# Decay attention with a squared-ReLU MLP: whole heads' reciprocals through POOL's queue, division one unit sooner, and another pace of weight conversion

## The chip, the cores and the metric

The kernel runs on one core of a Trainium2 chip. The metric is the device time of the program in microseconds (us), as the median of several runs; less is better. The core has five engines with instruction queues of their own, each worked off in order: PE (matrix products), DVE (vector), ACT (scalar functions), POOL (GpSimd) and SP, which here only issues DMA transfers.

## The reference, cut to what matters

```python
def _attn_ref(q, k, v, f):            # (8, 8, 576, 64), f: (8, 8, 576)
    scores = np.matmul(q, k.transpose(0, 1, 3, 2)) / np.sqrt(D)
    cum = np.cumsum(np.log(np.clip(f, 0.0001, 1.0)), axis=-1)
    scores = np.where(causal, -1e9, scores + cum[..., :, None] - cum[..., None, :])
    scores = scores - np.max(scores, axis=-1, keepdims=True)
    attn = np.exp(scores)
    attn = attn / (np.sum(attn, axis=-1, keepdims=True) + 1e-09)
    return np.matmul(attn, v)
...
x = attn_out.transpose(0, 2, 1, 3).reshape(8 * 576, 512)
h = np.maximum(x @ w_in, 0.0)         # w_in: (512, 2048), float64
return (h * h @ w_out)                # w_out: (2048, 512), float64
```

There are 8 batches of 8 heads, so 64 heads of 576 positions, and an MLP over 4608 rows.

## The kernel before

**Units.** Each head is cut into 6 *units* (a block of keys against a range of queries). The 384 units, numbered n = 0 to 383, are written out in one long loop, which starts at n = -12 to prepare. In unit n the loop writes the scores and the exponential of that unit (PE, then ACT, line 409), the product with the values of the unit two before (PE, lines 435 to 437 or 456), and then whatever falls due in that unit. The row maxima of the next head (PE line 346, DVE line 354) are among this. `in_order` at the end fixes the order of tracing on PE, ACT, DVE and POOL, so each engine works in exactly this order. SP's queue is left to the order in which its transfers are written.

**Whole and split heads.** The first 14 heads (`NWHOLE`, units 0 to 83) are "whole": their operands stay float32, and PE passes over each matrix product several times. The others are "split" into a high and a low part of reduced precision, which costs work on DVE (lines 313, 314, 332, 425), ACT (line 424) and POOL (lines 321, 324, 333, 411) and saves PE passes.

**Division.** The sum of each row's exponentials comes out of the value product as one more row. Two heads (a pair) share a tile `den` of 128 partitions. `finish` divides in four parts: part 0 loads the two rows from `den` into the compact tile `cmp` (128 partitions by 9), part 1 forms the reciprocal on DVE and stores it to a DRAM tile `rdr`, part 2 spreads each head's 576 reciprocals over its 64 partitions of `den` with two transfers, and part 3 multiplies the tile `xt` with `den` on POOL (line 492). All transfers are on SP's queue. `DIVIDE` says how many units behind the pair's last unit each part is written: 2, 5, 8 and 11 for the first 8 heads, and 2, 4, 6 and 7 for the others.

**Conversion of weights.** The MLP's 32 weight tiles arrive as float64. `weight_ops` turns each into a float32 and then a high and a low part, in four steps per tile: `tensor_scalar` on DVE (line 228); `tensor_scalar` on DVE (line 233) and the high part of the tile before on ACT (line 210); `scalar_tensor_tensor` on DVE (line 236), the low part of the tile before on POOL (line 216) and the magnitude of the next on ACT (line 205); `scalar_tensor_tensor` on DVE (line 240) and the next loads on SP (line 194). There are 132 steps. `RATES` says how many steps a unit gets: 1 in units -12 to -7, 1.6 in -3 to -1, 0.8 from unit 0 to `ready[0]`, and 2 behind it. The tile `osb` that a conversion writes has two buffers, so line 233 of a tile waits until POOL has read the tile two before.

**MLP.** `ready[b]` is the unit from which batch b's rows may be used, two behind the division of its last pair. `split_x` (DVE lines 509 and 510) splits 256 rows at a time. `fill` writes the MLP's steps between the units, each step in two halves: `mlp1` (12 products on PE, line 522, then ACT lines 530 and 532, DVE lines 531 and 533) and, for the step before, `mlp2` (6 products on PE, line 545). The 64 halves of the first two chunks are spread evenly up to `ready[1]`, which is 104. A step can only be written once its two weight tiles are converted; when chunk 0 lacks weights, chunk 1 goes on with those that are there. Once the last tile is converted, the halves that are left are spread anew.

Of the kernel before, what the change touches and what calls it, by code (L numbers as in the profile page):

```python
# [34 lines left out]
def decay_attention_relu2_kernel(  # L35
# [18 lines left out]
    nc = tc.nc  # L54

    NH, D, _, S = qk.shape
# [17 lines left out]
    NWHOLE = 14  # L74
# [8 lines left out]
    def bank(use):  # L83
# [11 lines left out]
        out=mz[:, MW - P:], in_=mz[:, MW - P:], pattern=[[-1, P]],  # L95
# [6 lines left out]
        out=eye, in_=eye, pattern=[[-1, P]],  # L102
# [370 lines left out]
    def finish(h, part):  # L473

        st = state[h]
        den = st["den"]
        if part == 0:
            st["cmp"] = wk.tile([P, S // D], F32, name="cmp")

            for i in range(2):  # L480
                nc.sync.dma_start(out=st["cmp"][i * D:(i + 1) * D], in_=den[i * D:i * D + 1, :])
        if part == 1:
            nc.vector.tensor_scalar_add(st["cmp"], st["cmp"], EPS)
            nc.vector.reciprocal(out=st["cmp"], in_=st["cmp"])
            st["rdr"] = dr.tile([2, S], F32, name="rdr")
            nc.sync.dma_start(out=st["rdr"].rearrange("h (p c) -> (h p) c", p=D), in_=st["cmp"])
        if part == 2:
            for i in range(2):
                nc.sync.dma_start(out=den[i * D:(i + 1) * D], in_=st["rdr"][i:i + 1].broadcast_to([D, S]))
        if part == 3:  # L490
            x = xts[h // H][:, (h % H) // 2, :]
            nc.gpsimd.tensor_tensor(out=x, in0=x, in1=den, op=ALU.mult)
            del state[h], state[h - 1]
# [97 lines left out]

    RATES = (1, 1.6, 0.8, 2)
    LAG = 2
    NA = H * NU


    DIVIDE = (2, 5, 8, 11), (2, 4, 6, 7)
    MAXIMA = (0, 0.5, 1, 1.5, 2, 2.5), (1.5, 2, 2.5, 3, 3.5, 4)  # L600
    SPLIT = 0, 1, 1, 3
    LOAD = 4
# [9 lines left out]
    def fin(h, part):  # L612

        return (h + 1) * NU - 1 + DIVIDE[h >= H][part]

# [33 lines left out]
    def cv(k):  # L649
        owed[0] += k  # L650
        convert(int(owed[0]))
        owed[0] -= int(owed[0])
# [52 lines left out]
    for n in range(-2 * NU, last_slot + 1):  # L705
        live = 0 <= n < len(slots)
        split_last()
        if live:
            h, u = slots[n]
            score(h, u)  # L710
            if h >= NWHOLE:
                unsplit.append((h, u))
        for ha, ua in avs.get(n, ()):
            if ua < NU - 1:
                av_part(ha, ua, False)
            else:
                av_part(ha, ua, True)
                av_part(ha, ua - 1, True)
        for args in fins.get(n, ()):
            finish(*args)  # L720
        for do in events.get((n, 0), ()):
            do()
        wr = RATES[0] * (n < -NU) if n < -NU // 2 else RATES[1 if n < 0 else 2 if n < ready[0] else 3]
        cv(wr / 2)
        fill(n, 0.5)
        for do in events.get((n, 1), ()):
            do()
        cv(wr / 2)
        fill(n, 1.0)
# [44 lines left out]
```

## Time and profile before

| | |
|---|---|
| time, median of 3 runs | 1230.48 us (1229.43 to 1232.88) |
| the profiled execution | 1229.0 us, span 1227.3 us |
| PE busy | 1187.9 us, 97% of the span |
| PE weight loads busy | 1047.9 us, 85% |
| DVE busy | 781.5 us, 64% |
| ACT busy | 710.3 us, 58% |
| POOL busy | 376.4 us, 31% |
| DMA | 71.88 MB, mean 59 GB/s |

A profile's "busy" is the time in which the engine has an instruction under way; overlapping instructions count once. PEclk is the share of full speed that the TensorE clock was granted. In a list of groups, "x12 | 15.5, 1290 | 22.4 <-ACT w L210 22.4" means: twelve instructions, 15.5 us busy, 1290 ns mean, 22.4 us idle on this engine just before them, and what ended the idle time. In a timeline a row is the start, the duration, the engine, the line, the operation and its tiles.

### The profile page before, as it was taken

The page shows a single profiled execution, that of the slowest core. Times are in us where ns is not written, and L with a number is a line of the kernel's source. Part 1 is how long each engine was busy: PE and PEld are TensorE (multiplying, and loading weights), DVE is VectorE, ACT ScalarE, POOL GpSimd, SP SyncE. Part 2 cuts the span into 40 slices and gives each one's busy share as a digit, 9 for nine tenths or more (in the row PEclk, how much of TensorE's full clock was granted, in tenths as well). Part 3 has the DMA queues.
Part 4 walks back from the last instruction along what each step waited for, and adds up shares of the span by engine and source line. Part 5 has one row for each costly group of instructions (what it writes and reads, how often), then busy time and mean ns, then how long its engine had stood idle before and what let it go on. Part 6 is the DMA issues. An engine that isn't in the chain of part 4 may idle for free.

```text
span 1227.3 us, 23243 instructions
## 1 busy us (share of the span) xinstructions
PE 1187.9 (97%) x7770; PEld 1047.9 (85%) x7770; DVE 781.5 (64%) x2046; ACT 710.3 (58%) x1748; POOL 376.4 (31%) x566
## 2 busy tenths in 40 slices
PE   6997998899999999999999999999999999999998
PEld 3665877788999899999999989998999899999997
DVE  5767778876666767666665666767666667533322
ACT  2774655556666666665656666666666666533232
POOL 3332234533333333332322243333333433200000
PEclk8998999899999999999999999999999999999999
DMA  7777501121221212111111121211111212000000
GB/s 216 209 187 178 185 16 33 25 70 34 48 50 41 59 41 53 37 44 36 49 19 56 26 59 42 58 41 45 38 52 41 59 41 59 11 28 1 18 18 18
DMA packets 106376, 71.88 MB, mean 59 GB/s; under 512 B 88184, under 2 KB 88184, under 8 KB 106256
## 3 DMA queue, kind: packets, MB, share of 16 engines
q1 hardware_dynamic: 105136, 66.26, 21.0%
q0 software_dynamic: 1120, 4.13, 1.4%
q8 instruction: 62, 1.02, 0.4%
q14 instruction: 58, 0.48, 0.1%
HBM read 60.20 MB, written 9.88 MB: 57 GB/s over the span
## 4 chain that ended last, share of the span: by engine, by line
PE 76%; ACT 2%; issue 2%; POOL 1%; DVE 0%; DVEq 0%; POOLq 0%
PE bank L522 30%; PE bank L545 28%; PE bank L435 3%; PE bank L437 3%; PE bank L402 3%; PE bank L436 3%; PE bank L346 3%; PE bank L399 3%; POOL v L333 0%; ACT den L471 0%; ACT p L409 0%; ACT r L530 0%; ACT ph L424 0%; ACT gh L532 0%; POOL p L411 0%
## 5 line engine op out<-in xcount | busy, mean ns | idle before, releaser
L545 PE MATMUL bank<-w,gh 128*128 128x512 f32 x1152 | 412.9, 399 | 0.0
L522 PE MATMUL bank<-xh,w 128*128 128x256 f32 x2304 | 331.5, 287 | 5.5 <-DVE tcol L354 5.5
L522 PEld LDWEIGHTS bank<-xh,w 128*128 128x128 f32 x2304 | 303.5, 191 | 13.2 <-DVE tcol L354 5.9
L425 DVE TENSOR_TENSOR pl<-p,ph 128x320 fp32r<-128x320 f32 (+4 forms) x300 | 186.0, 620 | 196.9 <-ACT ph L424 191.4
L545 PEld LDWEIGHTS bank<-w,gh 128*128 128x128 f32 x1152 | 217.1, 188 | 38.1
L530 ACT ACTIVATE r<-bank 128x256 f32<-128x256 f32 x288 | 110.3, 383 | 220.3 <-PE bank L522 200.3
L545 PE MATMUL bank<-w,gl 128*128 128x512 f32 x576 | 226.8, 394 | 0.1
L531 DVE TENSOR_TENSOR g<-r 128x256 f32<-128x256 f32 x288 | 128.5, 446 | 139.0 <-ACT r L530 138.3
L411 POOL TENSOR_SCALAR_AFFINE_SELECT p<-p 128x128 f32<-128x128 f32 (+1 forms) x250 | 83.6, 334 | 423.6 <-ACT p L409 322.7
L424 ACT CAST ph<-p 128x320 fp32r<-128x320 f32 (+4 forms) x300 | 124.4, 415 | 152.3 <-POOL p L411 110.2
L522 PE MATMUL bank<-xl,w 128*128 128x256 f32 x1152 | 185.6, 284 | 0.0
L522 PEld LDWEIGHTS bank<-xl,w 128*128 128x128 f32 x1152 | 159.3, 192 | 0.0
L533 DVE TENSOR_TENSOR gl<-g,gh 128x256 fp32r<-128x256 f32 x288 | 134.4, 467 | 35.7 <-DVE g L531 0.9
L409 ACT ACTIVATE p<-bank 128x320 f32<-128x320 f32 (+4 forms) x300 | 115.9, 386 | 62.7 <-PE bank L402 51.2
L354 DVE CUSTOM_DVE_ANT_0 bank<-bank,mz 128x256 f32<-128x256 f32 (+4 forms) x320 | 133.5, 432 | 27.4 <-PE bank L346 23.3
L346 PE MATMUL bank<-rk 66*128 66x320 f32 (+4 forms) x384 | 112.5, 318 | 22.0 <-DVE tcol L354 13.4
L532 ACT ACTIVATE gh<-r 128x256 fp32r<-128x256 f32 x288 | 120.4, 418 | 9.2
L545 PEld LDWEIGHTS bank<-w,gl 128*128 128x128 f32 x576 | 109.0, 189 | 14.3 <-DVE gl L533 0.9
L346 PEld LDWEIGHTS bank<-rk 66*128 66x128 f32 (+1 forms) x384 | 68.2, 182 | 40.1 <-DVE tcol L354 16.5
L435 PE MATMUL bank<-pl,vh 128*65 128x320 f32 (+4 forms) x350 | 97.6, 279 | 4.6 <-ACT den L471 4.6
L436 PE MATMUL bank<-ph,v 128*64 128x320 f32 (+4 forms) x350 | 95.2, 272 | 0.0
L437 PE MATMUL bank<-ph,vh 128*65 128x320 f32 (+4 forms) x350 | 93.8, 274 | 0.0
(85 smaller groups left out, 1523.5 us busy)
## 6 DMA issues: line engine op xcount, KB each, us to landing
qkraw<-in_qk SPq DMA_DIRECT2D x50, 288.0 KB
v<-in_v SPq DMA_DIRECT2D x64, 160.0 KB
den<-rdr SPq DMA_DIRECT2D x64, 144.0 KB
out<-osb SPq DMA_DIRECT2D x36, 256.0 KB
w<-in_w_in SPq DMA_DIRECT2D x16, 512.0 KB
w<-in_w_out SPq DMA_DIRECT2D x16, 512.0 KB
rl<-in_qk SPq DMA_DIRECT2D x14, 288.0 KB
rk<-in_qk POOLq DMA_DIRECT2D x14, 288.0 KB, 5.0
```

The lines of the kernel that those rows point to most:

```text
L346: nc.tensor.matmul(ps[:m, :n], st["r2"][:D + 2, q0:q0 + m], st["kl0"][:D + 2, k0:k0 + n], start=True, stop=True,)
L354: nc.vector.tensor_tensor_reduce(out=ps[:m, :n], in0=ps[:m, :n], in1=mz[:m, mo:mo + n], op0=ALU.add, op1=ALU.min, scale=-1.0, scalar=init, ...
L424: nc.scalar.copy(out=ph[:kn, :n], in_=p[:kn, :n])
L425: nc.vector.tensor_tensor(out=pl[:kn, :n], in0=p[:kn, :n], in1=ph[:kn, :n].bitcast(F32), op=ALU.subtract,)
L435: nc.tensor.matmul(acc[:D + 1, o], vh, pl[:kn, i], start=first, stop=False)
L436: nc.tensor.matmul(acc[:D, o], vl, ph[:kn, i], start=False, stop=False)
L437: nc.tensor.matmul(acc[:D + 1, o], vh, ph[:kn, i], start=False, stop=last)
L522: nc.tensor.matmul(ph[:, :T], w[:, s, cc], x[:, cc, :], start=(cc == 0 and k == 0), stop=(cc == NCC - 1 and k == 2),)
L531: nc.vector.tensor_tensor(out=g, in0=r, in1=r, op=ALU.mult)
L532: nc.scalar.activation(out=gh, in_=r, func=AF.Square)
L533: nc.vector.tensor_tensor(out=gl, in0=g, in1=gh.bitcast(F32), op=ALU.subtract)
L545: nc.tensor.matmul(po, g[:, ts], w[:, s], start=(fc == 0 and k == 0), stop=(fc == NF - 1 and k == 2),)
```

## The change

`finish` takes POOL's queue instead of SP's for the store of part 1 and the two transfers of part 2, for the 14 whole heads (7 pairs). For the first 8 heads parts 1, 2 and 3 are written one unit sooner: 4, 7 and 10 units behind the pair's last. With this `ready[0]` goes from 60 to 59, and so do the split of the first rows and the MLP's first step. Conversion gets 1.1 steps a unit from unit 0 to 58 and 2.3 from unit 59.

```diff
@@ finish
         den = st["den"]
+        queue = nc.gpsimd if h < NWHOLE else nc.sync
...
-            nc.sync.dma_start(out=st["rdr"].rearrange("h (p c) -> (h p) c", p=D), in_=st["cmp"])
+            queue.dma_start(out=st["rdr"].rearrange("h (p c) -> (h p) c", p=D), in_=st["cmp"])
         if part == 2:
             for i in range(2):
-                nc.sync.dma_start(out=den[i * D:(i + 1) * D], in_=st["rdr"][i:i + 1].broadcast_to([D, S]))
+                queue.dma_start(out=den[i * D:(i + 1) * D], in_=st["rdr"][i:i + 1].broadcast_to([D, S]))
...
-    RATES = (1, 1.6, 0.8, 2)
+    RATES = (1, 1.6, 1.1, 2.3)
...
-    DIVIDE = (2, 5, 8, 11), (2, 4, 6, 7)
+    DIVIDE = (2, 4, 7, 10), (2, 4, 6, 7)
```

Lines behind 476 carry a number that is one higher in the changed kernel. By the rates, the 132 steps end in unit 95 before (1 ahead of the loop, 10.8 up to unit -1, 48 in units 0 to 59, the other 72.2 at 2) and in unit 83 now (1, 10.8, 64.9 in units 0 to 58, the other 55.3 at 2.3).

**Ahead of the MLP's first step.** On POOL before, heads 6 and 7 (the last pair of batch 0, tile `den_914`) leave one row; `w..` are weight tiles, `rk` is a head's rounded operands, `v` its values.

```order
L216 TENSOR_TENSOR w11_1051<-osb_970,w11_1051 128x512
L216 TENSOR_TENSOR w12_1135<-osb_1049,w12_1135 128x512
L303 MEMSET v_1154 128x5x2
L287 DMA rk_0_79<-in_qk 64x1152
L492 TENSOR_TENSOR xt0_333<-xt0_333,den_914 128x576
L216 TENSOR_TENSOR w13_1213<-osb_1133,w13_1213 128x512
```

On POOL now, the same pair (`den_953`):

```order
L487 DMA rdr_1111<-cmp_1074 128x9
L287 DMA rk_1_80<-in_qk 64x1152
L216 TENSOR_TENSOR w15_1117<-osb_1040,w15_1117 128x512
L490 DMA den_953<-rdr_1111 64x576 x2
L216 TENSOR_TENSOR w16_1170<-osb_1115,w16_1170 128x512
L303 MEMSET v_1202 128x5x2
L493 TENSOR_TENSOR xt0_340<-xt0_340,den_953 128x576
```

The store stands ahead of a load of operands and a low part, the spread ahead of another low part, and the division behind it; four more weight tiles have been converted by then.

**At the first split head's units.** On DVE before, around unit 84; the last chunk of conversion stands between the work of the split heads (`pl<-p,ph`, `rk<-qkraw`) and of the MLP (`g`, `gl`).

```order
L531 TENSOR_TENSOR g<-r 128x256
L533 TENSOR_TENSOR gl<-g,gh 128x256
L228 TENSOR_SCALAR wmag<-wmag 128x512
L233 TENSOR_SCALAR osb<-wmag 128x512
L425 TENSOR_TENSOR pl<-p,ph 128x320
L313 CAST rk_80<-qkraw 64x576
L314 CAST rk_80<-qkraw 64x576
L236 SCALAR_TENSOR_TENSOR osb<-w_1899,osb 128x512
L531 TENSOR_TENSOR g<-r 128x256
L533 TENSOR_TENSOR gl<-g,gh 128x256
L240 SCALAR_TENSOR_TENSOR osb<-w_1899,osb 128x512
```

On DVE now, at the same place:

```order
L532 TENSOR_TENSOR g<-r 128x256
L534 TENSOR_TENSOR gl<-g,gh 128x256
L425 TENSOR_TENSOR pl<-p,ph 128x320
L532 TENSOR_TENSOR g<-r 128x256
L534 TENSOR_TENSOR gl<-g,gh 128x256
L313 CAST rk_80<-qkraw 64x576
L314 CAST rk_80<-qkraw 64x576
L354 ISA bank_2289,tcol<-bank_2289,mz 128x256
```

The four conversion rows have gone from here and from the eleven units behind; they stand between the whole heads' maxima now.

## The prediction

> **What bounds the kernel now.** I read the page first: engines, then the slices.
>
> ```profile
> PE 1187.9 (97%) x7770; PEld 1047.9 (85%) x7770; DVE 781.5 (64%) x2046; ACT 710.3 (58%) x1748; POOL 376.4 (31%) x566
> PE   6997998899999999999999999999999999999998
> PEclk8998999899999999999999999999999999999999
> ```
>
> PE bounds the program. The change takes nothing from PE, so it can only win idle PE time and clock, and both are missing in the first 9 slices alone. So I cut that part by unit: the exponentials of line 409 give the start of units 0, 60, 66, 84, 96 and 108 at 26.9, 105.3, 131.9, 192.2, 240.5 and 278.7 us. The first row below counts 61 of them (units 0 to 59, and one at the edge).
>
> ```profile
> 26.90:105.30 78.40, 23.28 (x61) 1.00 0.79 201
> ```
>
> All engines in these stages:
>
> ```profile
> core 0: us, PE busy (x) PEld busy (x) DVE busy (x) ACT busy (x) POOL busy (x), PEclk, DMA share, GB/s
> 26.90:105.30 78.40, 73.86 (x415) 48.50 (x414) 56.98 (x175) 56.79 (x141) 25.94 (x35) 1.00 0.79 201
> 105.30:131.90 26.60, 20.77 (x123) 17.12 (x121) 18.72 (x40) 11.63 (x29) 5.89 (x7) 0.87 0.67 185
> 131.90:192.20 60.30, 58.22 (x357) 47.66 (x356) 44.96 (x103) 33.73 (x82) 19.97 (x17) 1.00 0.24 74
> 192.20:240.50 48.30, 41.10 (x246) 36.09 (x245) 41.19 (x87) 27.83 (x68) 24.41 (x27) 0.93 0.13 30
> 240.50:278.70 38.20, 34.54 (x223) 30.95 (x224) 27.03 (x67) 22.60 (x58) 14.56 (x21) 0.96 0.20 57
> 278.70:311.10 32.40, 32.03 (x221) 29.22 (x220) 22.04 (x61) 20.71 (x53) 11.87 (x19) 1.00 0.19 40
> 311.10:1227.30 916.20, 910.49 (x6133) 829.62 (x6131) 556.85 (x1485) 530.34 (x1316) 264.94 (x414) 1.00 0.16 40
> ```
>
> Behind 278.7 us PE idles 6 us in 949, and the order there doesn't change. Two stages lose much: units 60 to 65 (the MLP's start) and units 84 to 95 (the first two split heads), where DVE is busy 41.19 of 48.3 us.
>
> **Units 84 to 95.** Two steady split heads take 32.4 us (row 278.70) with 16 MLP halves. Here 17.5 halves are due by the code (64 x 12/44), and the chain of waits prices a half:
>
> ```profile
> 1035.20 1.47 PE bank L545 x6
> 1037.06 1.50 PE bank L522 x12
> ```
>
> So PE needs 32.4 + 1.5 x 1.5 = 34.6 us and takes 48.3: 13.7 us are lost. The groups of DVE in this stage name the cause:
>
> ```profile
> L240 DVE SCALAR_TENSOR_TENSOR osb<-w,osb 128x512 int32<-128x512 int32 x6 | 7.8, 1292 | 0.1
> L236 DVE SCALAR_TENSOR_TENSOR osb<-w,osb 128x512 int32<-128x512 int32 x6 | 4.1, 676 | 0.0
> L228 DVE TENSOR_SCALAR wmag<-wmag 128x512 f32<-128x512 f32 x6 | 3.6, 604 | 0.0
> L233 DVE TENSOR_SCALAR osb<-wmag 128x512 int32<-128x512 int32 x6 | 3.5, 591 | 0.1
> ```
>
> Six weight tiles are converted here: 7.8 + 4.1 + 3.6 + 3.5 = 19.0 of DVE's 41.2 us. The new rates end the conversion in unit 83, so DVE keeps 22.2 us of work, as in the steady row (22.04). The nearest rows for what loss stays are the steady stage (0) and units 96 to 107, without conversion but with the banks of this stage: 38.2 - 34.6 = 3.6 us. I take 3, nearer to the second, whose banks are the same. Gain: 13.7 - 3 = **10.7 us** (10.1 to 13.7).
>
> The stage behind (240.5) has a clock of 0.96: 0.04 x 38.2 = **1.5 us**, which I count as won too, since it is the tail of the idle time ahead of it (0 to 3.6).
>
> **What the six tiles cost where they go.** Units 0 to 58 get 0.3 x 59 / 4 = 4.4 tiles more, and units 59 to 83 the other 1.6. The price of a tile in units 0 to 59:
>
> ```profile
> L216 POOL TENSOR_TENSOR w<-osb,w 128x512 fp32r<-128x512 f32 x12 | 15.5, 1290 | 22.4 <-ACT w L210 22.4
> L236 DVE SCALAR_TENSOR_TENSOR osb<-w,osb 128x512 int32<-128x512 int32 x12 | 14.6, 1221 | 0.2
> L346 PE MATMUL bank<-rk 66*128 66x320 f32 (+4 forms) x60 | 21.1, 399 | 3.7 <-DVE p L354 3.5
> L240 DVE SCALAR_TENSOR_TENSOR osb<-w,osb 128x512 int32<-128x512 int32 x12 | 8.2, 680 | 0.1
> L228 DVE TENSOR_SCALAR wmag<-wmag 128x512 f32<-128x512 f32 x11 | 5.3, 485 | 0.0
> L233 DVE TENSOR_SCALAR osb<-wmag 128x512 int32<-128x512 int32 x12 | 5.0, 418 | 0.3
> ```
>
> The means add up to 1.22 + 0.68 + 0.49 + 0.42 = 2.80 us, so DVE gets 4.4 x 2.80 = 12.4 us more and goes from 57.0 to 69.4 of about 77 us: 90% busy. All of it could hide, or all of it could end on PE: 0 to 12.4 us. That 90% can hide, two heads of this stage show:
>
> ```profile
> 42.70:49.80 7.10, 7.01 (x42) 4.50 (x40) 6.48 (x19) 5.65 (x16) 2.41 (x5) 1.00 0.85 237
> 49.80:57.00 7.20, 7.19 (x43) 4.77 (x42) 6.35 (x17) 5.68 (x16) 1.84 (x2) 1.00 0.76 204
> ```
>
> DVE is busy 6.48 of 7.10 and 6.35 of 7.20 us while PE idles 0.1. But over the stage PE idles 78.4 - 73.9 = 4.5 us for 12 tiles, nearly all behind DVE's maxima (row L346): 0.38 us a tile, 4.4 x 0.38 = 1.7. To this come DVE's waits for `cmp`, whose load now has two units to land instead of three, in four pairs at up to half a microsecond. I take **4 us lost**, in the lower third since the nearest rows are those two heads. The 1.6 tiles behind unit 58 cost at the same rate (0.9 a tile) **1.5 us** (0 to 4.5, which is 1.6 x 2.80); DVE is busy 63.7 of 86.9 us there.
>
> **The MLP's start.** The timeline around 100 us:
>
> ```profile
> 96.03 0.22 DVE L484 RECIPROCAL cmp<-cmp 128x9 f32<-128x9 f32 x1
> ...
> 102.15 0.68 DVE L240 SCALAR_TENSOR_TENSOR osb<-w,osb 128x512 int32<-128x512 int32 x1
> 107.56 1.79 DVE L509 CAST xh<-xt 128x1024 fp32r<-128x1024 f32 x1 [4.74 <-POOL xt L492]
> ```
>
> POOL's and PE's sides of it, and SP's two transfers:
>
> ```profile
> 106.14 1.39 POOL L492 TENSOR_TENSOR xt<-xt,den 128x576 f32<-128x576 f32 x1 [4.05 <-DMA den<-rdr]
> ...
> 111.41 2.08 PE L522 MATMUL bank<-xh,w 128*128 128x256 f32 x8 [5.50 <-DVE tcol L354]
> ...
> 96.28 0.34 SPq L486 DMA_DIRECT2D rdr<-cmp  x1
> ...
> 99.37 1.11 SPq L489 DMA_DIRECT2D den<-rdr  x2
> ```
>
> The chain is: reciprocal 96.03, store, spread issued at 99.37, landed by 106.14, division, DVE stands 4.74 us before it may split the rows, PE idles 5.5. By the stage's row 5.8 us of idle time and about 2 us of halved clock are lost, 7.8 in all. Part 1 and the split both move one unit ahead, so only a shorter chain helps. On POOL's queue the trace has one kind of transfer:
>
> ```profile
> L287 POOL DMA_DIRECT2D rk<-in_qk x10 | 5.9, 593 | 20.6 <-PE bank L395 20.6
> ```
>
> ```profile
> rk<-in_qk POOLq DMA_DIRECT2D x14, 288.0 KB, 5.0
> ```
>
> It issues in 0.59 us and lands in 5.0, for as many bytes as both spreads of a pair. So: reciprocal to the store's landing 0.25 + 0.59 + 2.75 (as on SP, 96.62 to 99.37), spread 0.59 + 5.0: 9.2 us against 10.1 (96.03 to 106.14), 0.9 less; a DVE that is fuller comes later to the split, by some 1 us. The idle time falls from 5.5 to about 3.6, and I count **2.5 us** won with some clock (from -1.3, a unit's length, where the split comes sooner and the landing doesn't, to 7.8).
>
> What else moves hides: 21 transfers of 0.59 us on POOL are 12.4 us, between 45 and 215 us, where POOL is busy a third of the time; if that cover were gone, they would delay the low parts behind them (last rival). SP loses as many issues, and the loads behind them start sooner.
>
> The Trainium skill speaks against this part: its page "SBUF — State Buffer", section "Summary: rules for kernel authors", says that building the descriptors of a transfer issued by GpSimd is starved while DVE runs in its fast modes, and advises the SP or ACT queue. By the figures of that page's section "A bandwidth-pool intuition that's wrong" (620 ns alone, 3100 beside a copy) a pair's three transfers would take 7.4 us longer, as an estimate. The trace doesn't agree so far: 593 ns mean while DVE is busy 73%.
>
> **Sum.** 4 + 1.5 - 2.5 - 10.7 - 1.5 = -9.2 us. The profiled execution took 1229.0 us around a span of 1227.3, 1.5 below the median of 1230.48; I take the difference to the median: **1221.3 us**.
>
> **Rivals.**
> *DVE becomes the bound in units 0 to 58.* For it: row L236, held up by POOL's L216 to 1221 ns here against 676 in units 84 to 95. Against: the two heads at 90%. Price 12.4 instead of 4: 1229.7 us.
> *The start closes wholly and DVE has room.* -10.7 - 1.5 - 7.8 = -20.0: 1210.5 us. For it: the 0.1 us of idle; against: the landing of 5.0 us.
> *POOL's transfers go out late,* held up by DVE's operations. Each would wait for one at most 1.2 us (row L236), 3.7 us a pair, and the gain at the start turns into -1.3: 1225.1 us. Against it: the 593 ns. This is the Trainium skill's rule of "SBUF — State Buffer" above.
> *Slower: POOL's queue stands.* POOL now waits in order for the store's landing and then for the spread's, and the low parts (L216) stand behind them. `osb` has two buffers, so DVE may go on for three steps, 2.7 units or 3.6 us in the whole heads; then DVE stops, and PE behind it. Before, POOL stood as follows:
>
> ```profile
> POOL xt L492 <- DMA den<-rdr: 15.2, 6, 4.2
> ```
>
> That is 2.5 us in the mean and 4.2 at most, mostly within the slack. It decides once both waits together pass some 5 us in each pair: 7 pairs x 2.6 us = 18.2 more, 1239.5 us.
> *The conversion doesn't leave units 84 to 95* is out: the order shows it gone.
>
> **Chances and range.** Forecast 0.60, DVE the bound 0.12, start closed 0.10, late transfers 0.09, POOL stands 0.09. What differs by less than 0.3% (3.7 us) can't be told from no change here, so faster means below 1226.8: nearly all of the forecast, the third and the fourth case, a little of the second, 0.79. Same: most of DVE the bound, 0.12. Slower: 0.09. The range of 1211 to 1230 us leaves out the slower case, half of DVE the bound and half of the start closed, 0.2 in all.
>
> **What would show it.** In the profile after: units 84 to 95 near 37 us with DVE under 60% busy and no line 236 or 240 in them (right), or above 44 (wrong). Units 0 to 59 at 78 to 84 us; at 90 the second case holds. PE's idle time ahead of its first L522 at 2 to 4 us instead of 5.5. POOL's DMA rows near 0.6 us; at 1.5 they are starved. POOL's waits for `rdr` and `den` above 5 us a pair with L216 late would mean the slower case.

## The result, and the profile after

The changed kernel takes 1235.71 us (median of 11 runs, 1233.73 to 1246.26) against 1230.48 us for the kernel before: ratio 1.0057, 95% interval 1.0033 to 1.0082. It is slower; the forecast was 1221.3 us. The profiled execution took 1234.32 us, 5.3 more than the one before. Page of the changed kernel, engine PE, its slices and its clock:

```profile
PE 1194.8 (97%) x7770; PEld 1052.9 (85%) x7770; DVE 780.7 (63%) x2046; ACT 711.0 (58%) x1748; POOL 384.7 (31%) x587
PE   6997998989999999999999999999999999999998
PEclk7988998999999999999999999999999999999999
```

PE is busy 6.9 us longer for the same 7770 instructions: a lower clock. The digits of the clock change in the first 8 of the 40 slices alone. So here are the stages again, cut at the exponentials of units 0, 60, 66, 84, 96 and 108 (columns as in the prediction):

```profile
27.50:120.50 93.00, 82.20 (x427) 54.40 (x427) 71.71 (x198) 63.11 (x152) 41.05 (x53) 0.90 0.82 221
120.50:140.00 19.50, 19.50 (x115) 16.00 (x115) 18.02 (x40) 11.46 (x28) 6.37 (x8) 0.94 0.46 134
140.00:203.60 63.60, 59.85 (x356) 49.85 (x355) 51.35 (x105) 34.82 (x82) 23.84 (x23) 0.95 0.12 29
203.60:243.10 39.50, 36.78 (x236) 32.71 (x235) 21.93 (x63) 22.52 (x57) 13.88 (x22) 0.96 0.17 42
243.10:282.70 39.60, 36.15 (x231) 31.94 (x229) 26.07 (x65) 21.70 (x56) 13.10 (x19) 0.96 0.17 45
```

The MLP's first step now stands ahead of unit 60, so the first two stages are read together: 112.5 us against 105.0. The next lost 3.3 us, units 84 to 95 won 8.8, and units 96 to 107 lost 1.4. Three of POOL's waits between 20 and 245 us (in all, times, longest), then two groups of its issues, then the landings (the last number is the median time from issue to landing):

```profile
POOL xt L493 <- DMA den<-rdr: 17.8, 7, 4.0
POOL rdr L487 <- DVE cmp L485: 11.9, 5, 4.8
POOL den L490 <- DMA rdr<-cmp: 10.9, 4, 4.0
```

```profile
L490 POOL DMA_DIRECT2D den<-rdr x14 | 7.6, 549 | 11.0 <-DMA rdr<-cmp 10.9
L487 POOL DMA_DIRECT2D rdr<-cmp x7 | 4.5, 640 | 20.7 <-DVE cmp L485 11.9 <-DVE wmag L228 4.5 <-DVE osb L233 4.3
```

```profile
den<-rdr POOLq DMA_DIRECT2D x14, 144.0 KB, 3.6
rdr<-cmp POOLq DMA_DIRECT2D x7, 4.5 KB, 3.9
```

The issues cost what was counted, 0.55 and 0.64 us. But POOL now waits 10.9 us for the store's landing, a wait that it did not have, and still 17.8 us for the spread's (15.2 before). The store of 4.5 KB takes longer to land than the spread. Timeline at the MLP's start:

```profile
101.42 0.22 DVE L485 RECIPROCAL cmp<-cmp 128x9 f32<-128x9 f32 x1
...
101.94 0.57 POOL L487 DMA_DIRECT2D rdr<-cmp  x1 [4.33 <-DVE osb L233]
...
108.29 1.15 POOL L490 DMA_DIRECT2D den<-rdr  x2 [3.95 <-DMA rdr<-cmp]
...
113.51 1.40 POOL L493 TENSOR_TENSOR xt<-xt,den 128x576 f32<-128x576 f32 x1 [2.73 <-DMA den<-rdr]
...
114.94 0.69 DVE L510 CAST xh<-xt 128x1024 fp32r<-128x1024 f32 x1 [5.38 <-POOL xt L493]
...
115.78 0.55 PE L523 MATMUL bank<-xh,w 128*128 128x256 f32 x1 [4.68 <-DVE xh L510]
```

From the reciprocal's end (101.64) to the division (113.51) it takes 11.9 us, where the kernel before took 9.9 (96.25 to 106.14) for the same pair. I call this stretch *the chain* below. PE idles 4.68 us, nearly as long as before (5.50).

Three more stops of PE are new, in units 35, 80 and 91. Unit 35, timeline of POOL, DVE, ACT and PE:

```profile
71.00 1.05 POOL L490 DMA_DIRECT2D den<-rdr  x2 [3.26 <-DMA rdr<-cmp]
...
72.06 1.29 POOL L216 TENSOR_TENSOR w<-osb,w 128x512 fp32r<-128x512 f32 x1
...
73.38 0.43 DVE L233 TENSOR_SCALAR osb<-wmag 128x512 int32<-128x512 int32 x1 [1.91 <-POOL w L216]
73.84 0.67 ACT L205 ACTIVATE wmag<-w 128x512 f32<-128x512 f32 x1 [2.37 <-DVE osb L233]
...
74.97 0.68 ACT L381 COPY rl<-bank 1x512 f32<-1x512 f32 x2
...
75.60 1.43 PE L392 MATMUL bank<-rl 67*128 67x320 f32 x2 [1.76 <-ACT rl L381]
```

POOL stands for the store, so the low part (L216) is late, so DVE finds no free `osb`, so ACT's magnitude and the copy behind it are late, so PE stops. What this costs is not the 1.76 us but the clock. In windows of the same run, the 3.4 us with the stop and the stretch behind:

```profile
71.80:75.20 3.40, 2.04 (x15) 1.28 (x13) 1.75 (x4) 1.33 (x3) 1.59 (x3) 1.00 0.81 200
75.20:85.40 10.20, 9.80 (x28) 6.51 (x29) 5.18 (x20) 5.11 (x13) 4.63 (x5) 0.50 0.72 210
```

Half the clock for 10.2 us is 5.1 us lost, as an estimate; units 24 to 47, which hold this stop alone, took 36.9 us against 31.9 in rates_div, the changed kernel on SP's queue (below). The Trainium skill, page "TensorE: Matmul & The Clock Gate", section "What's actually happening", says that the clock is set by activity in windows of 3.4 us; the halved stretches of this trace behind unit 0 last 3.4, 6.8 and 10.2 us, which agrees. Here PE was busy 2.04 us in the window of 3.4 us ahead of the halving. That share alone doesn't decide: in the kernel before, PE was busy 2.05 us between 262.1 and 265.5 us, and the clock stayed whole behind it.

Unit 80, POOL's and DVE's rows and the first of PE's behind them:

```profile
180.43 1.41 POOL L493 TENSOR_TENSOR xt<-xt,den 128x576 f32<-128x576 f32 x1 [2.73 <-DMA den<-rdr]
...
181.80 1.74 POOL L216 TENSOR_TENSOR w<-osb,w 128x512 fp32r<-128x512 f32 x1
...
183.54 1.54 POOL L321 TENSOR_TENSOR rl<-qkraw,rk 64x576 fp32r<-64x576 f32 x1
...
183.97 2.63 DVE L534 TENSOR_TENSOR gl<-g,gh 128x256 fp32r<-128x256 f32 x1
...
185.05 1.26 POOL L216 TENSOR_TENSOR w<-osb,w 128x512 fp32r<-128x512 f32 x1
186.39 1.46 POOL L324 TENSOR_TENSOR rl<-qkraw,rl 64x576 fp32r<-64x576 f32 x1
186.52 1.61 DVE L228 TENSOR_SCALAR wmag<-wmag 128x512 f32<-128x512 f32 x1
...
188.58 0.63 PE L346 MATMUL bank<-rk 66*128 66x320 f32 x1 [3.75 <-DVE tcol L354]
```

The division waited, and with it the four tensor operations behind it; then POOL ran the five without a break from 180.43 to 187.85. Beside them DVE's operations, 0.43 and 0.42 us elsewhere (L534 at 178.33, L228 at 193.70), took 2.63 and 1.61, each ending just behind one of POOL's; the maxima came late and PE idled 3.75 us. The Trainium skill, page "SBUF — State Buffer", section "Who interferes with whom", says that a DVE instruction with two inputs in SBUF and a GpSimd instruction that reads SBUF block each other for a whole instruction, whichever starts second. The row of L534 agrees; L228 has one input, so this sentence doesn't cover it.

Unit 91, the division of the last whole pair and the stop of PE behind it:

```profile
226.18 1.42 POOL L493 TENSOR_TENSOR xt<-xt,den 128x576 f32<-128x576 f32 x1 [3.49 <-DMA den<-rdr]
...
230.93 0.61 PE L346 MATMUL bank<-rk 66*128 66x320 f32 x2 [2.29 <-DVE tcol L354]
```

Behind the division stands a split head's mask (line 411, at 227.59), for which ACT's cast waited 1.65 us and, behind that, DVE's `pl` 2.71 us; the maxima behind `pl` came late. In rates_div POOL reached the division of this pair with its `den` already landed, and PE's idle time there is 0.44 us.

### The profile page after: what moved, and what is told of

It is laid out like the page before. It is cut to its first block, busy times and chain, and to the rows that moved or that the text cites. A ratio compares the mean times of both kernels' runs of the same rounds, so it can differ in the third digit from the quotient of the medians.

```text
span 1232.6 us, 23298 instructions
## 1 busy us (share of the span) xinstructions
PE 1194.8 (97%) x7770; PEld 1052.9 (85%) x7770; DVE 780.7 (63%) x2046; ACT 711.0 (58%) x1748; POOL 384.7 (31%) x587
## 5 line engine op out<-in xcount | busy, mean ns | idle before, releaser
L532 DVE TENSOR_TENSOR g<-r 128x256 f32<-128x256 f32 x288 | 125.9, 437 | 133.0 <-ACT r L531 132.6
L534 DVE TENSOR_TENSOR gl<-g,gh 128x256 fp32r<-128x256 f32 x288 | 132.2, 459 | 36.1 <-DVE g L532 0.9
L346 PE MATMUL bank<-rk 66*128 66x320 f32 (+4 forms) x384 | 115.4, 325 | 21.6 <-DVE tcol L354 17.3
L546 PEld LDWEIGHTS bank<-w,gl 128*128 128x128 f32 x576 | 109.6, 190 | 14.3 <-DVE gl L534 0.9
```

The costliest lines, as they stand in the source:

```text
L346: nc.tensor.matmul(ps[:m, :n], st["r2"][:D + 2, q0:q0 + m], st["kl0"][:D + 2, k0:k0 + n], start=True, stop=True,)
L532: nc.vector.tensor_tensor(out=g, in0=r, in1=r, op=ALU.mult)
L534: nc.vector.tensor_tensor(out=gl, in0=g, in1=gh.bitcast(F32), op=ALU.subtract)
L546: nc.tensor.matmul(po, g[:, ts], w[:, s], start=(fc == 0 and k == 0), stop=(fc == NF - 1 and k == 2),)
```

## The experiments

Each kernel was timed beside the kernel before on the same chip; the kernels are spread over several chips, on which the median of the kernel before lay between 1230.5 and 1231.1 us, so the medians are compared with each other too. The *chain* is worked out from each kernel's profiled execution: start of the division's row (L493 of the changed kernel) less the end of the reciprocal's (L485), mean of the 7 pairs. It is one execution a kernel, and not always one near the median: stand_sp's took 1237.51 us, rates_queue's 1243.06, queue_div's 1248.03, late_sp's 1226.84 and osb4's 1230.56.

| kernel | what it is | median us | ratio (95%) | chain us |
|---|---|---|---|---|
| before | | 1230.5 | | 8.6 |
| rates_only | before, new rates | 1222.76 | 0.9927 (0.9904 to 0.9950) | 8.0 |
| rates_div | changed, SP's queue | 1222.16 | 0.9925 (0.9902 to 0.9949) | 8.3 |
| rates_queue | changed, old DIVIDE | 1238.59 | 1.0057 (1.0032 to 1.0083) | 11.5 |
| queue_div | changed, old rates | 1244.65 | 1.0092 (1.0066 to 1.0118) | 10.5 |
| store_pool | changed, spread on SP | 1229.15 | 0.9978 (0.9962 to 0.9994) | 8.9 |
| spread_pool | changed, store on SP | 1233.32 | 1.0012 (1.0000 to 1.0025) | 10.7 |
| late_pool | changed, parts later | 1227.88 | 0.9981 (0.9961 to 1.0001) | 12.3 |
| late_sp | the same on SP's queue | 1222.15 | 0.9933 (0.9907 to 0.9958) | 9.6 |
| osb4 | changed, four `osb` | 1234.21 | 1.0033 (1.0011 to 1.0056) | 9.9 |
| stand_sp | rates_div, POOL waits | 1225.58 | 0.9964 (0.9942 to 0.9986) | 8.8 |
| issue_pool | rates_div, POOL issues | 1223.36 | 0.9942 (0.9921 to 0.9962) | 8.6 |
| stand_issue | rates_div, both | 1223.75 | 0.9957 (0.9939 to 0.9975) | 8.7 |
| stand_busy | rates_div, POOL waits and fills | 1233.24 | 1.0017 (1.0005 to 1.0029) | 10.4 |
| hop_sp | rates_div, one hop more | 1234.98 | 1.0034 (1.0019 to 1.0048) | 11.3 |
| cmp_late | rates_only, part 1 later | 1222.29 | 0.9929 (0.9904 to 0.9955) | 8.1 |

### Which of the three edits

The theories of these four: Q, POOL's queue costs; R, the denser conversion costs more than was counted; D, writing the parts a unit sooner costs.

**rates_only**: of the change only

```diff
-    RATES = (1, 1.6, 0.8, 2)
+    RATES = (1, 1.6, 1.1, 2.3)
```

> The kernel before with the new rates of conversion alone (store and spread on SP, division as before). Theory Q (POOL's queue stands behind the store's landing and makes DVE wait for osb): the loss in units 0 to 59 stays under 2 us, the 9 us of units 84 to 95 are won, 1221 to 1225 us. Theory R (the denser conversion itself stops PE): units 0 to 59 lose 5 to 8 us and units 78 to 83 some 5 as in the changed kernel, 1231 to 1236 us. Theory D (parts 1 to 3 a unit sooner leave the cmp load too little time): as Q, 1222 to 1226 us.

Measured 1222.76 us, 7.7 less than before: R falls.

**rates_div**: the changed kernel with `queue = nc.sync`.

> The changed kernel with store and spread back on SP's queue. Q: 1221 to 1226 us, PE's stop near unit 35 and near unit 80 both gone. R: 1232 to 1237 us, both still there. D: DVE still waits for cmp, 1231 to 1236 us.

Measured 1222.16 us: D falls too: on SP's queue the sooner parts cost nothing that can be told. Its stages, cut at the same units:

```profile
26.40:115.00 88.60, 80.34 (x429) 52.78 (x427) 68.40 (x198) 63.30 (x153) 34.72 (x42) 0.94 0.74 192
115.00:133.60 18.60, 18.33 (x115) 15.01 (x114) 17.78 (x41) 11.62 (x28) 4.68 (x5) 1.00 0.72 218
133.60:193.70 60.10, 57.82 (x357) 47.49 (x355) 49.30 (x106) 34.96 (x81) 22.77 (x20) 1.00 0.26 70
193.70:230.60 36.90, 35.42 (x236) 31.32 (x235) 22.91 (x63) 22.52 (x57) 12.07 (x19) 1.00 0.17 44
230.60:270.20 39.60, 36.14 (x230) 31.93 (x229) 26.08 (x65) 21.67 (x56) 13.12 (x19) 0.96 0.18 46
```

Against the changed kernel every stage up to unit 95 is shorter, by 4.4, 0.9, 3.5 and 2.6 us, the clock is higher in each, and the stop at unit 80 is gone (no idle time of PE above 1.1 us there). The pair ahead of the MLP, DVE, SP and POOL:

```profile
98.37 0.22 DVE L485 RECIPROCAL cmp<-cmp 128x9 f32<-128x9 f32 x1
...
98.61 0.34 SPq L487 DMA_DIRECT2D rdr<-cmp  x1
...
102.35 1.11 SPq L490 DMA_DIRECT2D den<-rdr  x2
...
106.19 1.40 POOL L493 TENSOR_TENSOR xt<-xt,den 128x576 f32<-128x576 f32 x1
```

Chain 7.6 us instead of 11.9; from the store's issue to the spread's 3.74 instead of 6.35.

**rates_queue**: the changed kernel with the old first tuple, `DIVIDE = (2, 5, 8, 11), (2, 4, 6, 7)`.

> The changed kernel with the division's parts where they were before (5, 8 and 11 units behind). Q: POOL still waits for the store's landing, but three units lie between store and spread as in the changed kernel, so 1231 to 1236 us. R: 1231 to 1236 us. D: 1222 to 1226 us, without DVE's wait for cmp.

Measured 1238.59 us, 2.6 above the range of Q. Beside rates_only, the queue costs 15.8 us with the old places. The MLP's start in the profiled execution:

```profile
115.05 1.13 POOL L490 DMA_DIRECT2D den<-rdr  x2 [7.10 <-DMA rdr<-cmp]
...
124.20 1.39 POOL L493 TENSOR_TENSOR xt<-xt,den 128x576 f32<-128x576 f32 x1 [6.21 <-DMA den<-rdr]
...
130.14 2.08 PE L523 MATMUL bank<-xh,w 128*128 128x256 f32 x8 [14.30 <-DVE tcol L354]
```

POOL stands 13.3 us for the two landings and PE 14.3 us.

**queue_div**: the changed kernel with the old `RATES = (1, 1.6, 0.8, 2)`.

> The changed kernel with the rates of before (store and spread on POOL, division a unit sooner). Q: the stop of PE by a late low part shows in some pair though conversion is thinner, and nothing is won behind: 1233 to 1240 us. R: no loss in units 0 to 59, 1228 to 1232 us. D: a loss of 2 to 4 us in units 0 to 59 by DVE's waits for cmp, 1232 to 1235 us.

Measured 1244.65 us, 4.7 above the range of Q: the queue loses time without denser conversion too (in the profiled execution PE stops 5.10 us in unit 27, behind an L216 that was 3.62 us late for DVE). Together, by the medians: the rates are worth -7.7 us on SP's queue and -8.9 on POOL's, the sooner parts -0.6 and -2.9, the queue +13.5 to +15.8. Of these the queue, and the rates on SP's queue, are clear of the noise. The sooner parts are not (on POOL's queue both kernels have the ratio 1.0057), and the intervals behind the -8.9 overlap.

### What of the queue: its transfers one by one, the places, the buffers

Theory B: POOL's standing in its order is the cost. Theory L: the transfers land later on POOL's queue.

**store_pool**: in part 2 only, `queue.dma_start` back to `nc.sync.dma_start`. **spread_pool**: the same in part 1 only.

> The changed kernel with the spread back on SP's queue; the store stays on POOL's. Two readings of POOL's cost are left. B (standing): POOL's low parts wait behind the spread's wait for the store, and DVE waits for them. L (landing): a transfer from POOL's queue lands later (3 to 7 us against 2 to 3 from SP), so every division is late. B: POOL no longer waits for the store's landing, 1222 to 1227 us. L: half of the lateness stays, and SP stands instead with the loads of operands behind it, 1227 to 1232 us.

> The changed kernel with the store back on SP's queue; the spread stays on POOL's and waits there for the store's landing. B: POOL stands for the store's landing, which is shorter from SP; some stops of PE stay, 1226 to 1232 us. L: only the spread lands late, 1225 to 1230 us.

Measured 1229.15 and 1233.32 us, so +7.0 and +11.1 on rates_div; both transfers together +13.5. The spread on POOL's queue is the worse one. The first speaks for L; the second lies above the ranges of both theories. From the store's issue to the spread's it takes 4.36 and 5.23 us in the mean, 5.27 in the changed kernel, 3.56 in rates_div.

**late_pool** and **late_sp**: the parts later, on POOL's and on SP's queue.

```diff
-    DIVIDE = (2, 4, 7, 10), (2, 4, 6, 7)
+    DIVIDE = (2, 4, 9, 14), (2, 4, 6, 7)
```

> The changed kernel with more units between the parts of the first 8 heads' division (4, 9 and 14 behind the pair's last unit instead of 4, 7 and 10), all on POOL's queue; the MLP's first step comes four units later. B: store and spread have landed before POOL comes to the wait, PE's stops in units 0 to 59 are gone, 1222 to 1229 us. L: as B in units 0 to 59; if instead the issue or the packets of POOL's transfers themselves slow the core, 1232 to 1237 us.

> Control of late_pool (1227.9 us): the same DIVIDE (2, 4, 9, 14), all transfers on SP's queue. Theory B: the queue still costs 3 to 6 us with late parts, since POOL still waits for the reciprocal: 1222 to 1225 us. Theory L: late parts hide the landing, so late_pool would already be as fast as SP: 1227 to 1229 us.

Measured 1227.88 and 1222.15 us: with two and four units more, the queue costs 5.7 us instead of 13.5. The time that is lost is one for which somebody waits, and later places take a part of it away. late_pool lies in the ranges of both theories, late_sp in that of B.

**osb4**: two more buffers for the first 16 tiles, in place of tiles that the MLP needs only later.

```diff
-            w = done[i] = wk.tile([P, DM], F32, name="osb")
+            if i < 16 and i % 4 > 1:
+                w = done[i] = wk.tile([P, 2 * DM], F32, name=("xh1", "xl1")[i % 2], bufs=1)[:, :DM]
+            else:
+                w = done[i] = wk.tile([P, DM], F32, name="osb")
```

> The changed kernel with four buffers in turn for the first 16 converted weight tiles instead of two, so that DVE no longer waits for the low part of the tile two before. B: DVE's waits for POOL ahead of line 233 are gone, and PE's stops in units 20 to 45 with them; POOL still stands, and the division ahead of the MLP's start stays late: 1226 to 1231 us. L: little changes, 1232 to 1237 us.

Measured 1234.21 us; the interval overlaps that of the changed kernel, though no wait of DVE's line 233 for POOL is left. So the two buffers, seen at work in unit 35, are not what most of the loss goes through.

### Standing, issuing, or the chain

**stand_sp**: rates_div, with POOL waiting where it waits in the changed kernel.

```diff
+                nc.gpsimd.tensor_copy(out=wk.tile([P, 1], F32, name="look"), in_=st["cmp"][:, :1])
         if part == 2:
+            if h < NWHOLE:
+                nc.gpsimd.memset(st["cmp"][:, :1], 1.0)
```

> The transfers of part 1 and 2 on SP's queue (as in rates_div, 1222.2 us), but POOL stands at the same places of its order: a copy of one column of cmp behind the store (waits for the reciprocal) and a memset of that column ahead of the spread (waits for the store's landing). No POOL transfer is added. Theory B (POOL's standing is the cost): most of the 13.5 us between rates_div and after comes back, 1230 to 1236 us, with POOL's waits for cmp and rdr near 12 and 10 us up to unit 96. Theory L (later landing on POOL's queue is the cost): 1221 to 1225 us.

Measured 1225.58 us. Its profile is of an execution of 1237.51 us: its chain is 8.8 us, and yet it is as slow as the changed kernel. It loses 19.5 us against that of rates_div in units 0 to 47; the clock is at half for 34.1 us of these 83.0, the first time from 31.0 us on, behind a stop of PE of 1.23 us in unit 1, ahead of any division. So a single execution can lose as much without a longer chain, and what follows speaks of medians. Standing at these places costs about 3.4 us (the intervals of stand_sp and rates_div overlap), not 13.5: B as I had put it falls short.

**issue_pool**: rates_div, with three transfers of 2.3 KB a pair issued by POOL at the same places, which nothing waits for. Theories: S, POOL's order and time; T, the transfers on POOL's queue as such. **stand_busy**: stand_sp, with three fills of `den` on POOL (`nc.gpsimd.memset(den, 1.0)`) where the issues stand.

> rates_div (1222.2 us), all transfers of the division on SP's queue, with three more transfers of 2.3 KB a pair issued from POOL at the places of the store and the spread, from DRAM to DRAM, for which nothing waits and which wait for nothing of the pair. It adds the issuing alone, 21 times 0.55 us. Theory S: no more than 2 us, 1222 to 1225 us, since POOL has the room and does not stand. Theory T: a part of the 10 us that stand_sp does not explain, 1226 to 1232 us.

> stand_sp (1225.6 us) with POOL's time for issuing put back as work: one fill of den behind the wait of part 1 and two ahead of the spread, about half a microsecond each, as the three issues of a pair take in the changed kernel (0.53 to 0.71 us). Transfers stay on SP's queue. Theory S (what costs is POOL's order and time: its standing and what it does there, whatever issues the transfers): 1230 to 1236 us. Theory T (the transfers on POOL's queue themselves cost): as stand_sp, 1223 to 1228 us.

Measured 1223.36 us for issue_pool: 21 issues cost nothing that can be told from rates_div. The issues took 533 and 540 ns in the mean.

stand_busy took 1233.24 us, which spoke for S. But two things in it are not as in the changed kernel: DVE's lines 228 and 233 took 815 and 689 ns in the mean (560 and 574 in the changed kernel), and the spread, though on SP's queue, has to wait for the fills of the tile that it writes.

**stand_issue**: stand_sp and issue_pool in one, which has neither.

> stand_sp and issue_pool together: the division's transfers stay on SP's queue, POOL waits for the reciprocal and for the store's landing, and issues three transfers of 2.3 KB a pair at those places, for which nothing waits. Against the changed kernel only the landing of the division's own transfers is that of SP's queue. Theory S (POOL's order and time, 3.4 and 1.2 us alone, more together since what POOL has behind them is bunched): 1229 to 1235 us. Theory L (what is left is the later landing on POOL's queue, for which POOL stands longer): 1224 to 1228 us, the sum of both.

Measured 1223.75 us. POOL's waits in it:

```profile
POOL look L489 <- DVE cmp L485: 15.0, 7, 4.5
POOL xt L500 <- DMA den<-rdr: 13.4, 5, 4.3
POOL cmp L493 <- DMA rdr<-cmp: 3.4, 4, 1.6
```

S falls: POOL stands 15.0 us for the reciprocals, longer than in the changed kernel, and issues 21 transfers, and 1.6 us are lost by the medians (3.9 by the ratios, whose intervals overlap; four of the twelve executions took 1228.6 to 1232.8 us). What differs is the time that POOL stands for the landings: 3.4 and 13.4 us instead of 10.9 and 17.8. The table's last column says the same: with the new rates and the places 4, 7 and 10, the kernels with a chain of 8.3 to 8.8 us take 1222 to 1226 us, those with 9.9 to 10.7 (the changed kernel 10.2) take 1233 to 1236, and store_pool, 8.9, lies between. Theory C: the time follows the chain, whatever makes it long.

**hop_sp** tests C without POOL: rates_div, with the reciprocals copied once more on SP's queue ahead of the spread.

```diff
         if part == 2:
+            if h < NWHOLE:
+                hop = dr.tile([2, S], F32, name="hop")
+                nc.sync.dma_start(out=hop.rearrange("h (p c) -> (h p) c", p=D), in_=st["rdr"].rearrange("h (p c) -> (h p) c", p=D))
+                st["rdr"] = hop
```

> rates_div (1222.2 us), all transfers on SP's queue, POOL neither waits for them nor issues any, but the reciprocals take one hop more: part 2 copies them from the first DRAM tile to a second one, which the spread then reads. The chain from the reciprocal to the division on POOL gets some 2 us longer, as long as in the changed kernel (10.2 us a pair against 8.3 in rates_div). Theory C (the time follows this chain, whatever makes it long): 1231 to 1237 us. Theory S (it is POOL's place and time): 1222 to 1225 us. Between them if the chain is a part of it.

Measured 1234.98 us, as slow as the changed kernel (1235.71), with no transfer of the division on POOL's queue and no wait of POOL's added. Its chain is 11.3 us, and the one wait that POOL has for the division grew from 19.1 us in rates_div to

```profile
POOL xt L497 <- DMA den<-hop: 35.6, 7, 8.7
```

C holds for the medians, and the trace shows how the chain costs: POOL stands for the last landing in front of the division, and its low parts and, from unit 60, the MLP's rows stand behind. Once the whole way can be followed, from POOL to PE:

```profile
75.11 1.40 POOL L497 TENSOR_TENSOR xt<-xt,den 128x576 f32<-128x576 f32 x1 [6.80 <-DMA den<-hop]
...
80.50 0.35 PE L346 MATMUL bank<-rk 66*128 66x192 f32 x1 [2.15 <-DVE p L354]
```

Between them two low parts end at 79.55, and DVE's line 233 waits for the first of them (1.43 us) and runs 1.47 us beside the second; the maxima come late, and the clock is at half for 10.2 us behind. Units 36 to 47 took 22.4 us against 15.9 in rates_div, half of the loss.

Two limits remain. The equal totals are partly chance: in units 78 to 95 the changed kernel loses 6.2 us against rates_div and hop_sp 0.5, where the chains of its last two pairs are 7.0 and 11.1 us instead of 9.2 and 12.8; and store_pool has a stop of 3.57 us in unit 80 behind a chain of 7.2, so a long chain isn't the only way to one. The hop also keeps SP waiting once more a pair, so SP's loads may have a share in these 12.8 us. None shows in the trace: between 20 and 245 us no engine but POOL and SP waits for a landing other than that of `cmp`, and for this DVE waits less (1.5 us, 3.8 in rates_div).

**cmp_late**: rates_only with `DIVIDE = (2, 6, 8, 11), (2, 4, 6, 7)`, to spare DVE's wait for `cmp`.

> rates_only (1222.8 us) with part 1 four units behind part 0 instead of three: DIVIDE (2, 6, 8, 11), SP's queue. In rates_only and rates_div DVE stands 3.3 and 2.7 us for the load of cmp at units 52 and 53 with PE idle behind it. If that stand costs its length and some clock: 1218 to 1221 us. If the store's landing, now two units ahead of the spread, takes its place, or the idle time is won back ahead of the MLP anyway: 1222 to 1224 us.

Measured 1222.29 us, no better than rates_only (1222.76): DVE's wait for `cmp` ahead of the MLP is gone, and PE idles 6.8 us ahead of the MLP instead. No kernel tried goes below 1222; rates_only, rates_div, late_sp and cmp_late can't be told apart, and each beats both kernels, by 0.7% against before.

## Why the prediction was wrong

*Units 84 to 95* (-10.7): the mechanism was right. On SP's queue the stage took 36.9 us, a gain of 11.4, where "near 37" was named. In the changed kernel it took 39.5, a gain of 8.8, with DVE busy 21.93 us (56%); the difference of 2.6 is the stop in unit 91, behind POOL's wait for the spread.

*The clock behind* (-1.5): wrong, +1.4, and so on SP's queue. The reading of the tail was right: before, the clock was at half from 241.6 to 245.0 us, behind a stop of 2.20 us that begins in unit 95, and this stretch is gone. But another of 3.4 us took its place, behind a stop of 2.16 us at 266.8. Such a stop was there before too (2.17 us at 264.3) and halved nothing; it lay across two windows of 3.4 us (PE busy 2.05 and 2.42 us), and now lies within one (1.24). PE is also busy 1.6 us longer, with 231 groups of products instead of 223.

*Units 0 to 59 and the MLP's start* (+4 and -2.5): with the store and the spread on SP's queue they came to +2.2 together, against +1.5 forecast, and that they are so near is partly luck. Up to unit 47 the conversion cost 1.5 us for 3.6 tiles more, as priced (0.38 a tile). Units 48 to 59 lost 8.8: one stop of PE of 2.84 us, behind 2.69 us of DVE's waiting for `cmp` (up to half a microsecond a pair was counted), half the clock for 10.2 us behind it, and the MLP's first products, which now stand there. Units 60 to 65 won 7.9: the start closed, where 2.5 was counted. On POOL's queue it was +7.5 in all.

*Units 66 to 83* (+1.5): -0.2 on SP's queue, +3.3 on POOL's; what lies between them is the stop in unit 80 and the clock behind it. So on SP's queue the terms add up to -8.0, where -9.2 was forecast, and 1222.16 us lies 0.9 from the forecast of 1221.3.

*The step that failed* is the one on POOL's queue, at two places of the text. The first is the sum "reciprocal to the store's landing 0.25 + 0.59 + 2.75 (as on SP [...]), spread 0.59 + 5.0: 9.2 us". From the store's issue to the spread's it took 6.35 us, not 3.34, at the MLP's start, and 5.27 in the mean of the pairs; the spread itself was as priced (5.22 to the division, 5.59 counted). I had taken the time from SP's queue for that on POOL's, and let the spread leave the moment it could, though POOL has its place in an order for it. At the MLP's start it is the landing: POOL already stood at the spread, 3.95 us. In the last two whole pairs it is the order: the store had landed 3.3 and 4.8 us before POOL came to the spread, which stands there only one unit ahead of the division (6 and 7 of `DIVIDE`); on SP's queue these spreads left 1.44 and 2.55 us behind the store instead of 5.14 and 7.96. These two pairs make over half of the longer chain (7.5 of 13.2 us, net, over the seven), and the stops in units 80 and 91 stand behind them. The second is "What else moves hides: 21 transfers of 0.59 us". The issues do hide: issue_pool shows it. What doesn't is the chain that they begin: seven chains of 1.9 us more (10.2 against 8.3) cost 13.5 us, through the stops of PE and the clock behind them. From the exponential of unit 0 to that of unit 108, the changed kernel and then rates_div:

```profile
27.50:282.70 255.20, 234.48 (x1360) 184.91 (x1359) 189.08 (x469) 153.61 (x371) 98.23 (x125) 0.93 0.42 112
```

```profile
26.40:270.20 243.80, 228.05 (x1359) 178.53 (x1358) 184.47 (x470) 154.06 (x371) 87.37 (x105) 0.97 0.45 118
```

Of the 11.4 us between them PE is busy 6.4 longer over the same groups, at a clock of 0.93 instead of 0.97, and idles 5.0 more.

*The rivals.* "POOL's queue stands" named the right side, and 1239.5 us was 3.8 too many. Its mark, more than 5 us a pair for the two landings, was not quite met ((17.8 + 10.9) / 7 = 4.1); 5.8 is reached only with the wait for the reciprocal (11.9), which the rival didn't name. I gave it 0.09, since I held POOL's waits against the slack of `osb` alone. Of its mechanism, the wait for the reciprocal costs little (stand_issue), the wait for landings is the cost (hop_sp), and `osb` is one way among four (unit 35; the others are the MLP's start, the bunch in unit 80 and the mask in unit 91). "DVE the bound" is out: on SP's queue a tile more cost as little as counted, not 2.8 us. "The start closes wholly" came about on SP's queue, without its 1210.5 us. "Late transfers", the Trainium skill's rule on page "SBUF — State Buffer", section "Summary: rules for kernel authors", that transfers issued by GpSimd starve beside DVE: the issues took 549 and 640 ns (3100 is the figure of its section "A bandwidth-pool intuition that's wrong"), and issues without a wait cost nothing that can be told from noise. But an issue's row doesn't show when the packets go out: the store ahead of the MLP sent its first 3.39 us behind its issue, with DVE busy 3.34 us of that time, while the other six took 1.28 to 1.75. Whether DVE held it up no run here shows. The advice, the SP queue, was right; what is shown as the reason is the later go of the spread and of the division, by landing and by POOL's order.

## What to carry to other kernels

Before a transfer goes to another engine's queue, price the whole chain to the instruction that waits for its landing, with landing times from that queue and with the place in that engine's order; the issue is the small part. An engine that is busy 31% has room for work, but not for any wait: what stands behind one can come late and then in a bunch. To find which of an edit's costs is real, build each alone on the old queue (the wait, the issue, the longer chain); the two that looked likeliest cost 3.4 and 1.2 us, neither clear of the noise, the third 12.8.

## What the runs showed of the hardware

A chain of small transfers is slower on POOL's queue, and less by the packets than by what stands around them. Over the seven pairs the last packet of the store ended 2.76 us behind its issue in the mean on POOL's queue (the changed kernel) and 2.47 on SP's (rates_div). In the pair ahead of the MLP it is worst: issue at 101.94, first packet at 105.33, last packet's end at 106.57, and POOL goes on at 108.29. In the four pairs in which POOL stood for the store, it went on 1.47 to 1.79 us behind the last packet; on SP's queue the spread of the pair ahead of the MLP left 1.03 us behind it.

One stop of PE of 1.76 us was followed by half the clock for 10.2 us, and the units around it took 5.1 us longer than in rates_div.

A `tensor_scalar` on DVE (line 228) takes longer beside POOL's work. Of its 30 rows in stand_busy, the 13 without POOL beside them took 418 ns in the mean, the 7 beside a fill 948, the 10 beside a `tensor_tensor` of POOL's 1240. In stand_issue, with issues of transfers in the place of the fills, the mean of all 30 was 542.
